# Opening of a spectral mixing and SoLU kernel: the last unit's rows, three weight loads, one conversion and the idle products are rearranged

## The chip, the cores and the metric

The kernel runs on one core of a Trainium2 chip. The metric is the device time of one execution in microseconds, as the median of five runs. The profile is of one execution of its own; its times count from the first instruction.

## The reference

Two blocks follow each other. The first filters a sequence in the frequency domain, along the sequence axis; the second is a feed-forward layer with a SoLU activation and a layer norm, over all 25088 tokens.

```python
# x: (8, 3136, 256); filt_r, filt_i: (1569, 256)
X = np.fft.rfft(x, axis=1)
Y = X * (filt_r + 1j * filt_i)[None]
y = np.fft.irfft(Y, n=3136, axis=1).reshape(25088, 256)
# w_in: (256, 1024), w_out: (1024, 256), g_ln: (1024,); both weights are float64 in memory
h = y @ w_in
e = np.exp(h - h.max(-1, keepdims=True))
solu = h * e / (e.sum(-1, keepdims=True) + 1e-9)
mu, var = solu.mean(-1), solu.var(-1)
out = (solu - mu) / np.sqrt(var + 1e-6) * g_ln @ w_out
```

## The kernel before

The Fourier transform of 3136 points is split into 49 x 64. For a batch element e there are four steps. `first` multiplies the rows by a 98 x 100 table and stores the result in DRAM (d1). `forward` (tile pb, line 300 and product at 292) takes two pairs of residues at a time, called a unit; the filter is applied in `multiply` (lines 313 to 315); `inverse` (tile pc) goes back, is evacuated by ScalarE (line 330) and stored in DRAM (d2, line 334). `back` (lines 353 and 356, tile py) loads rows of d2 as tile t4, multiplies by the table wi_t and leaves tokens in the large tile y. Batch element 0 has seven units, 0 to 6. Units 0 to 5 have four residues each; unit 6 has one residue, so its result is 128 x 256 elements, which are four rows (96 to 99) of t4.

Batch element 0 goes through all four steps in the opening (lines 360 to 560). The main loop (`step`, line 896) then runs over the token blocks: it multiplies tokens by w_in, takes the softmax, transposes, multiplies by w_out, and does the Fourier steps of the next batch elements beside it, at places that PLAN (line 37) names. The opening and the main loop are under a manual schedule: every engine runs its instructions in the order in which the code emits them, and so does each engine's DMA queue: SyncE (SP), ScalarE (ACT) and GpSimd (POOL) issue transfers. An issue on SP or ACT also waits until an earlier transfer that used the same completion semaphore has landed; eight of them go round.

What stands in the opening around the change:

- Weights. `begin(j)` issues the load of one eighth of the weights on POOL's queue (line 369, 512 KB of float64 words), j = 0 to 3 for w_in and 4 to 7 for w_out, into one of five buffers (tile raw). `convert(j)` makes float32 of it: a row of VectorE operations (lines 381 to 396), and for j below 4 also one multiplication on ScalarE (line 400) and two operations on POOL (401 and 405); for j from 4 on lines 403 on VectorE and 405 on POOL. `weight_sums` (line 141, VectorE) needs all four eighths of w_in.
- Units. The loop at line 524 emits, for unit i: the forward of unit i + 2, its multiply (real part on VectorE alone, imaginary part with its last operation, line 315, on POOL), two idle products (line 530), the inverse, and the store of the unit on ACT's queue. The tiles pr, pi, pt and g have two buffers each.
- Idle products (`idle`, line 492) write a PSUM tile that nobody reads; a row of 14 of them, tile idler, follows the last unit.
- Rows. The row loads of the step back (eight pieces, tile t; lines 172 and 173) are all issued on SP: 96 rows and 4 rows apart for each piece. After them SP issues the rows of batch element 1 (line 420, tile y), the copy of the filter to DRAM (line 548, f_dram), and then what the main loop gives it. POOL reads f_dram back at line 598, in the main loop.
- POOL makes the sums of a token pair for the main loop at line 658 (tile s), which the products on PE (line 680, tile m) need.

Of the kernel before, what the change touches and what calls it, by code (L numbers as in the profile page):

```python
# [9 lines left out]
FP32 = mybir.dt.float32  # L10
# [7 lines left out]
P = 128  # L18
B, S, C = 8, 3136, 256
# [5 lines left out]
NH = N2 // 2  # L25
# [3 lines left out]
NK = 4 * NS  # L29
NCH = 4  # L30
# [62 lines left out]
def kernel(  # L93
# [10 lines left out]
    nc = tc.nc  # L104
# [6 lines left out]
    def pool(name, bufs, space=None, stack=ctx):  # L111
        kw = {} if space is None else {"space": space}
        return stack.enter_context(tc.tile_pool(name=name, bufs=bufs, **kw))
# [7 lines left out]
    d2 = [dram.tile([NS, P, C], FP32, name=f"d2_{e}") for e in range(B)]  # L121
# [28 lines left out]
    def filter_rows(filt, quarter, u, i0, n):  # L150

        s0 = 2 * i0 + u
        off, step = (s0 * C, 2 * C) if quarter == 0 else ((N1 - s0) * C, -2 * C)
        return bass.AP(tensor=filt.tensor, offset=filt.offset + off,
                       ap=[[N1 * C, 32], [step, n], [1, C]])

    def all_filter_rows(i0, n):

        for k, filt in enumerate((filt_r, filt_i)):
            for u in range(2):  # L160
                for quarter in range(2):
                    held = min(n, (NS - u + 1) // 2 - i0)
                    yield (slice(NQ * u + 32 * quarter, NQ * u + 32 * quarter + 32), k, held,
                           filter_rows(filt, quarter, u, i0, held))

    def whole(dmas, out, in_):
        dmas[0](out=out, in_=in_)

    def by_16(dmas, out, in_):

# [164 lines left out]

    t4s = {}

    def fetch_back(e, ch, rows_pool, split=None):

        split = split or whole  # L340
        if rows_pool is not None:
            t4s[e, ch] = rows_pool.tile([P, NCH, C], FP32, name=f"t4_{e}_{ch}", tag="r")[0:NK]
        split(
            (nc.sync.dma_start if split is by_16 else nc.gpsimd.dma_start, nc.sync.dma_start), t4s[e, ch],
            d2[e].rearrange("s (a n) c -> (s a) n c", a=4)[:, NCH * ch:NCH * ch + NCH, :])

    def back(e, ch, cb, evac):

# [11 lines left out]
    with ExitStack() as st:  # L360
        fpool = pool("fp", 1, stack=st)
        pools = {name: pool(name + "0", bufs, stack=st)
                 for name, bufs in (("r", 1), ("t2", 1), ("p", 2), ("g", 2))}
# [3 lines left out]
        def load_words(src, n):  # L367
            raw = wpool.tile([P, 512, 2], I32, name=f"raw_{n}", tag="raw")
            nc.gpsimd.dma_start(
                out=raw.rearrange("p (k d) w -> p k d w", d=src.shape[-2]) if len(src.shape) == 4 else raw,  # L370
                in_=src)
            return raw
# [70 lines left out]
        def resident(held):  # L443
            def find(sp, u):
                i, pairs = sp.units[u]
                tile, at = held[i]
                return tile[:, at:at + pairs]
            return find

        sp = Spectrum(0, pools, resident(filters), resident(tables))  # L450
        raws = {}

        def begin(j):
            raws[j] = load_words(weights[j][1], j)
# [16 lines left out]
        pieces = NH // NCH  # L471
# [18 lines left out]
        def idle(out):  # L490

            nc.tensor.matmul(out=out, lhsT=tables[0][0][:, 0, 0].rearrange("p u q -> p (u q)"),
                             rhs=filters[0][0][:, 0], start=True, stop=True)

        def idle_row(count, name):
            for j in range(count):
                idle(ps_h.tile([P, 2, C], FP32, name=f"{name}_{j}", tag="h"))
# [3 lines left out]
        def convert(j):  # L501
            load_float64(weights[j][0], raws.pop(j), negate=j < 4, share=j < 4)
# [4 lines left out]
        def start(i):  # L507
            sp.fetch_filter(i)
            sp.fetch_de(i)
            sp.forward(i, halves(f"pb_0_{i}"))  # L510

        units = len(sp.units)

        sp.t2s[0] = t2_0 = pools["t2"].tile([P, 4, C], FP32, name="t2_0_0", tag="t2")
        for n in range(16):
            (nc.sync, nc.scalar)[n % 2].dma_start(
                out=t2_0[NH * (n % 4):NH * (n % 4) + NH, n // 4, :], in_=rows_x[n:n + 1])
# [6 lines left out]
        for i in range(units):  # L524
            if i + 2 < units:
                start(i + 2)
            sp.multiply(i, 0, nc.vector.tensor_tensor)
            sp.multiply(i, 1, nc.gpsimd.tensor_tensor)
            pss = [ps_t.tile([P, 2, C], FP32, name=f"pc_0_{i}_{u}", tag="t") for u in range(2)]
            idle(pss[0])  # L530
            sp.inverse(i, pss)
            sp.store(i, nc.scalar.dma_start)
            if i == 0:
                nc.gpsimd.dma_start(out=wi_t, in_=wi_dram)
                nc.gpsimd.dma_start(out=wq_t, in_=wq_dram)
                nc.gpsimd.dma_start(out=g_sb, in_=moe_g_ln.rearrange("(k p) -> p k", p=P))
            elif i != 2:
                begin({1: 2, 3: 3, 4: 4, 5: 5, 6: 6}[i])
        idle_row(14, "idler")
        rows_t4 = pools["r"].tile([P, NH, C], FP32, name="t4_0", tag="r")  # L540
        for ch in range(pieces):
            t4s[0, ch] = rows_t4[0:NK, NCH * ch:NCH * ch + NCH]
        for ch in range(pieces):
            fetch_back(0, ch, None, by_16)
        fetch_second()
        for i0, n, rows in ((0, 4, P), (4, 4, P), (8, NP - 9, P), (NP - 1, 1, NQ)):
            f, at = filters[i0]
            nc.sync.dma_start(
                out=f_dram[i0:i0 + n].rearrange("i u q k c -> (u q) i (k c)")[0:rows],
                in_=f[0:rows, at:at + n].rearrange("p i k c -> p i (k c)"))  # L550
        convert(2)
        begin(7)
        convert(3)
        convert(4)
        weight_sums(w_in_sb)
        for j in (5, 6, 7):
            convert(j)
        for ch in range(pieces):
            for cb in range(KD):
# [16 lines left out]
    pools = dict(f=pool("fp1", 2))  # L576
# [257 lines left out]
    for e in range(1, B):  # L834
        first_at, spectrum_at, back_at = PLAN[e]
        sp = Spectrum(e, pools, load_filter, load_de)
        if e == 1:
            sp = second
            sp.load, sp.load_de = load_filter, load_de
        for i, t in enumerate(first_at):  # L840
            dma = nc.gpsimd.dma_start
            if e == 1:
                if i not in sp.xs:
                    row_loads.append((t, t - 1, -1, lambda sp=sp, i=i, dma=dma: sp.fetch_x(i, [dma] * 2)))
                for u in range(2):
                    (early, late)[u][t].append(lambda sp=sp, i=i, u=u: sp.first(
                        i, (u,), psum(f"pa_{sp.e}_{i}_{u}").rearrange("p a c -> p (a c)").rearrange(
                            "p (o n) -> p o n", o=1), nc.scalar.copy, sp.xs[i][0:NK, 2 * u:2 * u + 2, :]))
                    (early, late)[u][t].append(lambda sp=sp, i=i, u=u: sp.store_first(
                        i, 2 * u, nc.gpsimd.dma_start))  # L850
            else:

                row_loads.append((t, t - 2, -1, lambda sp=sp, i=i: sp.fetch_quarters(i, nc.sync.dma_start)))
                stores[t].append(lambda sp=sp, i=i: sp.difference(i))
                products[t].append(lambda sp=sp, i=i: sp.sum(i))
                late[t].append(lambda sp=sp, i=i: sp.first_quarters(
                    i, [psum(f"pa_{sp.e}_{i}_{g}") for g in range(2)]))
                stores[t + 1].append(lambda sp=sp, i=i, dma=dma: sp.store_quarters(i, dma))
        for i, t in enumerate(spectrum_at):

            other = e == 1 and i % 2 == 1 and t + 1 < LAG
            add = nc.gpsimd.tensor_tensor if t + 1 < LAG else nc.vector.tensor_tensor


            dma = nc.sync.dma_start if e == 1 else nc.scalar.dma_start
            ahead(t, 2).append(lambda sp=sp, i=i, dma=dma: sp.fetch(i, dma))
            ahead(t, 1 if e == 1 and i % 2 == 1 else 2).append(lambda sp=sp, i=i: sp.fetch_filter(i))
            ahead(t, 2).append(lambda sp=sp, i=i: sp.fetch_de(i))
            early[t].append(lambda sp=sp, i=i, o=other: sp.forward(i, psum_pair(f"pb_{sp.e}_{i}", o)))
            late[t].append(lambda sp=sp, i=i, add=add: sp.multiply(i, 0, add))  # L870
            products[t + 1].append(lambda sp=sp, i=i, add=add: sp.multiply(i, 1, add))
            late[t + 1].append(lambda sp=sp, i=i, o=other: sp.inverse(i, psum_pair(f"pc_{sp.e}_{i}", o)))
            stores[t + 2].append(lambda sp=sp, i=i: sp.store(i, nc.gpsimd.dma_start))


        assert S * (e - 1) <= P * (back_at[0] // 2 * 2) and P * (back_at[-1] + 2) <= S * e // P // 2 * 2 * P
        for ch, t in enumerate(back_at):
            row_loads.append((
                t, t - 1, spectrum_at[-1] + 2, lambda e=e, ch=ch: fetch_back(e, ch, pools["r"])))
            for cb in range(KD):  # L880
                (early, late)[cb][t].append(
                    lambda e=e, ch=ch, cb=cb: back(e, ch, cb, nc.scalar.copy))
# [134 lines left out]
```

## Time and profile before

| what | value |
|---|---|
| median of five runs | 1684.33 us (1678.61 to 1685.2) |
| profiled execution, its own time | 1684.82 us |
| its span | 1683.0 us |
| mean granted TensorE clock | 0.988 |
| busy share: PE, DVE, POOL, ACT | 95%, 75%, 67%, 56% |
| PE busy in 0 to 100 us, and in 100 to 200 us | 71.70 us, 84.67 us |
| PE busy in 800 to 1000 us | 196.30 us |

Times in the profile are microseconds from the start of the span, where a line doesn't say ns. PE is the matrix engine, PEld its weight loads, DVE is VectorE, ACT is ScalarE, POOL is GpSimd; SPq, ACTq and POOLq are the sequencers that issue transfers. A line of the timeline has the start, the length, the engine, the line of the code, the operation, output and inputs by the program's names, shapes, how many were merged, and in brackets the idle time of the engine before it with what ended it. The chain of waits goes back from the last instruction, at each step to what released it. The page also cuts the span into 40 slices and writes the busy share of each as a digit.

### The profile page before, as it was taken

To read this page: it belongs to the slowest core of one execution; us is meant where nothing else is said; L and a number is where in the kernel's file an instruction comes from. 1 tells how busy PE (TensorE), PEld (TensorE's weight loads), DVE (VectorE), ACT (ScalarE), POOL (GpSimd) and SP (SyncE) were. 2 spreads that over 40 slices of the span, in tenths; PEclk is the share of its full clock that TensorE was granted. 3 is DMA by queue.
4 is the path that set the end of the run, shared out by engine and by line. 5 is a ranking of instruction groups with operands and counts; after the bars stand their busy time and mean duration, and the time that the engine had idled before them with its cause. 6 is when DMAs were issued, how large, how long until landed. Compare 5 with 4: busy or idle time off the path is not lost.

```text
span 1683.0 us, 31072 instructions
## 1 busy us (share of the span) xinstructions
PE 1599.5 (95%) x10022; PEld 1094.5 (65%) x10022; DVE 1267.4 (75%) x2619; ACT 939.4 (56%) x1730; POOL 1120.2 (67%) x1268
## 2 busy tenths in 40 slices
PE   5798899999999999999999999999999999999996
PEld 1353456756766677667666677667776777777776
DVE  1676787787787877887878878788778766777773
ACT  2154555656555556556565665556565666656651
POOL 4444777578666756787567866688566766666674
PEclk8998999999999999999999999999999999999999
DMA  9887768876788668865777658766776444444443
GB/s 256 247 268 223 230 195 228 215 212 173 194 230 227 184 181 232 228 184 147 202 230 211 179 151 229 226 183 173 196 210 170 116 126 123 100 109 103 112 112 96
DMA packets 375958, 311.72 MB, mean 185 GB/s; under 512 B 61515, under 2 KB 341572, under 8 KB 375796
## 3 DMA queue, kind: packets, MB, share of 16 engines
q1 hardware_dynamic: 306260, 169.81, 38.5%
q0 software_dynamic: 32640, 101.65, 20.5%
q10 hardware_dynamic: 36896, 38.28, 8.2%
q8 instruction: 81, 1.33, 0.3%
q14 instruction: 81, 0.66, 0.1%
HBM read 124.83 MB, written 81.50 MB: 123 GB/s over the span
## 4 chain that ended last, share of the span: by engine, by line
PE 64%; DMA 18%; DVE 8%; SPq 3%; issue 3%; POOL 2%; ACT 1%; ACTq 0%; DVEq 0%; POOLq 0%
PE m L680 25%; PE o L792 25%; DMA solu_t<-turn 8%; PE py L353 5%; SPq L750 2%; DMA x<-in_x_dram 2%; PE pc L292 2%; DMA t<-d 2%; PE pb L292 2%; PE pa L260 2%; DVE h L728 2%; DVE turn L738 1%; DMA out_dram<-ot 1%; DVE diff L245 1%; DMA y<-in_x_dram 1%
## 5 line engine op out<-in xcount | busy, mean ns | idle before, releaser
L730 ACT ACTIVATE e<-h,nmu 128x1024 f32<-128x1024 f32 x196 | 225.7, 1152 | 366.2 <-DVE h L728 364.2
L792 PEld LDWEIGHTS o<-w_out_sb,solu_t 128*128 128x128 f32 x3136 | 380.3, 192 | 59.3 <-issue 40.9
L792 PE MATMUL o<-w_out_sb,solu_t 128*128 128x128 f32 x3136 | 400.6, 276 | 10.2 <-DVE rsum L723 7.4
L680 PE MATMUL m<-w_in_sb,s 128*128 128x512 f32 x784 | 402.7, 605 | 6.1 <-ACT h L690 3.9
L792 PEld LDWEIGHTS o<-w_out_sb,u 128*128 128x128 f32 x2352 | 304.7, 191 | 147.1 <-issue 112.0
L658 POOL TENSOR_TENSOR u<-solu_t 128x512 f32<-128x512 f32 x98 | 145.5, 1484 | 306.1 <-DMA solu_t<-turn 186.3
L680 PE MATMUL m<-w_in_sb,y 128*128 128x512 f32 x588 | 313.1, 616 | 15.8 <-DVE nmax L704 11.9
L792 PE MATMUL o<-w_out_sb,u 128*128 128x128 f32 x2352 | 312.4, 276 | 6.8 <-ACT ot L804 5.8
L728 DVE SCALAR_TENSOR_TENSOR h<-e,rsum,h 128x1024 f32<-128x1024 f32 x196 | 291.1, 1485 | 6.9
L811 DVE SCALAR_TENSOR_TENSOR ot<-o,rs_t,ot 128x128 f32<-128x128 f32 x294 | 102.6, 349 | 202.4 <-ACT ot L804 166.6
L690 ACT COPY h<-m 128x512 f32<-128x512 f32 x294 | 173.9, 591 | 128.3 <-PE m L680 115.5
L738 DVE STREAM_TRANSPOSE turn<-h 128x1024 f32<-128x1024 f32 x196 | 242.3, 1236 | 0.8
L712 ACT ACTIVATE e<-h,nmax 128x1024 f32<-128x1024 f32 x196 | 226.5, 1155 | 0.0
L658 POOL TENSOR_TENSOR u<-solu_t,u 128x512 f32<-128x512 f32 x98 | 142.8, 1457 | 89.9 <-PE o L792 86.0
L704 DVE CUSTOM_DVE_ANT_0 h<-m,h 128x512 f32<-128x512 f32 x196 | 133.2, 680 | 78.2 <-ACT h L690 58.2
L680 PEld LDWEIGHTS m<-w_in_sb,y 128*128 128x128 f32 x588 | 94.9, 191 | 124.8 <-DVE nmax L704 65.6
L680 PEld LDWEIGHTS m<-w_in_sb,s 128*128 128x128 f32 x784 | 124.1, 191 | 67.6 <-issue 44.9
L356 ACT COPY y<-py 128x392 f32<-128x392 f32 x128 | 109.5, 856 | 104.7 <-PE py L353 102.9
L353 PEld LDWEIGHTS py<-wi_t,t 100*128 100x128 f32 x1024 | 132.2, 192 | 54.2 <-issue 40.5
L658 POOL TENSOR_TENSOR solu_t<-solu_t,solu_t 128x512 f32<-128x512 f32 x98 | 150.0, 1530 | 7.7
L658 POOL TENSOR_TENSOR u<-u,solu_t 128x512 f32<-128x512 f32 x98 | 136.2, 1390 | 0.7
L353 PE MATMUL py<-wi_t,t 100*128 100x98 f32 x1024 | 131.7, 273 | 0.7 <-DMA t<-d 0.4
(108 smaller groups left out, 1986.3 us busy)
## 6 DMA issues: line engine op xcount, KB each, us to landing
solu_t<-turn SPq DMA_DIRECT2D x784, 128.0 KB
out_dram<-ot SPq DMA_DIRECT2D x196, 128.0 KB
t<-d POOLq DMA_DIRECT2D x56, 400.0 KB, 5.0
d<-x POOLq DMA_DIRECT2D x100, 200.0 KB, 5.3
f<-f_dram POOLq DMA_DIRECT2D x39, 512.0 KB, 7.2
d<-g POOLq DMA_DIRECT2D x39, 512.0 KB, 5.3
t<-d ACTq DMA_DIRECT2D x36, 512.0 KB
x<-in_x_dram SPq DMA_DIRECT2D x112, 98.0 KB
```

What stands on the lines that cost most here:

```text
L353: nc.tensor.matmul(out=psv[:, i:2 * NCH - i:2 * NCH - 1 - 2 * i, :], lhsT=t4s[e, ch][:, i, cb * P:cb * P + P], rhs=wi_t, start=True, stop= ...
L356: evac(out=y[:, cb, t0:t0 + S].rearrange("p (r m j) -> p m j r", m=N2 // NCH, j=NCH)[:, ch:last + 1 - ch:last - 2 * ch], in_=psv.rearrange ...
L658: nc.gpsimd.tensor_tensor(out=out, in0=in0, in1=in1, op=op)
L680: nc.tensor.matmul(out=ms[j, bank], lhsT=lhsT, rhs=w_in_sb[:, w, :], start=m in (1, 2, 7), stop=True, skip_group_check=True)
L690: nc.scalar.copy(out=h_half(k, i), in_=ms[j, 0])
L704: nc.vector.tensor_tensor_reduce(out=h_half(k, i), in0=ms[j, bank], in1=h_half(*kept), scale=1.0, scalar=sofar, op0=ALU.add, op1=ALU.min, ...
L712: nc.scalar.activation(out=e, in_=hs[k], func=AFT.Exp, bias=nmaxs.pop(k)[:, 1:2], scale=-1.0, accum_out=esum)
L728: nc.vector.scalar_tensor_tensor(out=solu, in0=e, scalar=rsum, in1=solu, op0=ALU.mult, op1=ALU.mult, accum_out=nmu)
L730: nc.scalar.activation(out=e, in_=solu, func=AFT.Square, bias=nmu, scale=-float(DFF), accum_out=variances[g][:, i:i + 1])
L738: nc.vector.transpose(out=turns[g][:, :, i, :], in_=solus.pop(k).rearrange("p (f j) -> p f j", j=32))
L792: nc.tensor.matmul(out=pos[p, bank], lhsT=lhs[:, f, :], rhs=w[:, f, :], start=f == 0 and m in (1, 2, 7), stop=True, skip_group_check=True)
L811: nc.vector.scalar_tensor_tensor(out=ot, in0=pos[p, bank], scalar=rs, in1=out_half(p, *kept)[0], op0=ALU.mult, op1=ALU.add)
```

## The change

Six things are changed in the opening; the main loop is the same.

1. The store of unit 6 to DRAM is gone. Its four rows of t4 are written by four transfers straight from the tile g, each from 32 partitions into one row, two on ACT's queue and two on SP's.
2. The row loads of the step back are the 96-row ones alone, on SP behind those two.
3. Conversion 2 is emitted at the end of unit 2's turn, in place of after the row loads. Load 2 is issued at unit 0 and no longer at unit 1.
4. Loads 5, 6 and 7 are issued together after conversion 3. Before, 5 and 6 were issued at units 5 and 6, and 7 after conversion 2.
5. Conversion 4 comes after the weight sums and no longer before them; the loads of wi, wq and g come at unit 1 instead of unit 0.
6. The row of idle products has 9 instead of 14.

```diff
             idle(pss[0])
             sp.inverse(i, pss)
-            sp.store(i, nc.scalar.dma_start)
-            if i == 0:
+            if i + 1 < units:
+                sp.store(i, nc.scalar.dma_start)
+            if i in (0, 3, 4):
+                begin({0: 2, 3: 3, 4: 4}[i])
+            elif i == 1:
                 nc.gpsimd.dma_start(out=wi_t, in_=wi_dram)
                 nc.gpsimd.dma_start(out=wq_t, in_=wq_dram)
                 nc.gpsimd.dma_start(out=g_sb, in_=moe_g_ln.rearrange("(k p) -> p k", p=P))
-            elif i != 2:
-                begin({1: 2, 3: 3, 4: 4, 5: 5, 6: 6}[i])
-        idle_row(14, "idler")
+            elif i == 2:
+                convert(2)
+        idle_row(9, "idler")
         rows_t4 = pools["r"].tile([P, NH, C], FP32, name="t4_0", tag="r")
+        last = sp.gs.pop(units - 1)
+        for a in range(4):
+            (nc.scalar, nc.sync)[a % 2].dma_start(out=rows_t4[NK - 4 + a:NK - 3 + a],
+                                                  in_=last[NH * a:NH * a + NH, 0, :])
         for ch in range(pieces):
             t4s[0, ch] = rows_t4[0:NK, NCH * ch:NCH * ch + NCH]
-        for ch in range(pieces):
-            fetch_back(0, ch, None, by_16)
+            nc.sync.dma_start(
+                out=t4s[0, ch][0:NK - 4],
+                in_=d2[0].rearrange("s (a n) c -> (s a) n c", a=4)[0:NK - 4, NCH * ch:NCH * ch + NCH, :])
         fetch_second()
...
-        convert(2)
-        begin(7)
         convert(3)
-        convert(4)
+        for j in (5, 6, 7):
+            begin(j)
         weight_sums(w_in_sb)
-        for j in (5, 6, 7):
+        for j in range(4, 8):
             convert(j)
```

The function `whole` and the split of `fetch_back` go, since nothing else used them; for batch elements 1 to 7 `fetch_back` issues the same transfer as before.

## The prediction

> **What bounds the kernel now.** I read the page first: TensorE (PE) is busy for 95% of the span, and the 40 slices show a 9 for nearly all of it but the first four. The change touches only the opening, so I went to the table of 10 us windows for 0 to 200 us, where PE is busy for 156 of 200 us: there is slack there, and the question is which chain of waits holds it. Then I read the chain of waits over 55 to 120 us:
>
> ```profile
> 72.83 1.12 PE pc L492 x2
> 73.96 1.11 PE pc L292 x16
> 75.09 0.60 ACT g L330
> ...
> 78.88 1.12 PE pc L492 x2
> 80.01 0.58 PE pc L292 x4
> 80.59 12.21 PE idler L492 x28
> 92.80 1.09 PE py L353 x8
> ```
>
> The columns are start, length, work. A unit of the spectrum takes 2.9 to 3.1 us on PE (72.83 to 75.73 to 78.88); after the last one the 14 idle products run for 12.21 us (0.872 each), and the step back (py) starts at 92.80, the moment they end. They cover the row loads, which come late for this reason (first the waits of SyncE's queue, then the DMA queues in 80 to 84 us; the columns of the second are packets, MB and share of 16 engines):
>
> ```profile
> SPq L172 <- DMA d<-g: 21.1, 3, 10.6
> ```
> ```profile
> q0 software_dynamic: 220, 0.82, 77.4%
> q10 hardware_dynamic: 103, 0.10, 6.9%
> ```
>
> SP waits for the stores of the units. Unit 5's store is issued at 79.35, SP gets on at 88.03: 8.7 us, because in between GpSimd's queue (weight loads 5 and 6, issued at 77.03 and 78.89) moves 0.82 MB and the store's queue 0.10. From 88 us to 145 us the SP queue then always has work, and its end decides the next thing that stops PE, read in POOL's and PE's timelines:
>
> ```profile
> 141.12 0.74 POOL L598 DMA_DIRECT2D f<-f_dram  x1 [6.66 <-DMA f_dram<-f]
> 141.87 0.88 POOL L658 TENSOR_TENSOR s<-y 128x128 f32<-128x128 f32 x1
> ```
> ```profile
> 144.43 2.04 PE L680 MATMUL m<-w_in_sb,s 128*128 128x512 f32 x2 [3.27 <-ACT h L690]
> ```
>
> POOL waits 6.66 us for the filter's copy to DRAM (f_dram, line 548, behind the rows and the second batch element on SP's queue); its sums for the next token pair stand behind that, and PE waits 3.27 us. So the opening has two clocks: PE's (units, idle products, step back) and SP's DMA stream.
>
> **The change, part by part.** All times below are of the profiled execution: 1684.82 us, of which the span is 1683.0. It lies 0.49 above the median of the five runs (1684.33), so I add my sum to the median.
>
> *Conversion 2 between units 2 and 3.* It leaves VectorE's (DVE's) row behind unit 6 (77.95 to 82.50, 4.55 us) and enters a hole:
>
> ```profile
> 66.12 0.69 DVE L313 TENSOR_TENSOR pr<-pb,f 128x512 f32<-128x512 f32 x1 [6.91 <-PE pc L292]
> ```
>
> DVE idles 6.91 us up to 66.12. Load 2 is issued at 54.06 instead of 57.36; the six late loads land 4.5 to 8.4 us after issue, so at 58.6 to 62.5, and DVE is through by 63.8 to 67.1: nothing to 0.9 us late, taken as 0. But the conversion also has a multiplication on ScalarE (ACT, line 400, 0.69) and two operations on POOL (401 and 405, 1.46 and 1.35), and engines run them in the order written. ACT's one stands behind the evacuation and store of unit 2, and POOL's two stand ahead of unit 3's last operation (line 315):
>
> ```profile
> 70.29 0.37 ACTq L334 DMA_DIRECT2D d<-g  x1
> ```
> ```profile
> 69.48 1.27 POOL L315 TENSOR_TENSOR pi<-pi,pt 128x512 f32<-128x512 f32 x1 [8.86 <-DVE pt L314]
> ```
>
> So line 400 runs 70.70 to 71.39, 401 to 72.85, 405 to 74.2, and unit 3's line 315 ends at 75.4 instead of 70.75. PE's second half of inverse 3 (8 products, 1.09 us at unit 0) ends at 76.5, not 72.2: 4.3 us late. PE and DVE both need about 3 us a unit, so nothing is caught up. DVE's next pi also waits, since its pt buffer is freed by that line 315, and unit 5 waits for buffers of unit 3. On top, PE stands still from about 72.0 to 75.4. A gap of this kind is in the trace: 2.55 us before line 292 at 165.17, also waiting for POOL's pi, with a granted clock of 0.83 in 160 to 170 us; after 4.93 us of idling it was 0.71 in 60 to 70, where a pair of idle products took 2.00 instead of 1.05 and an inverse 1.87 instead of 1.04. That adds 0 to 2.5 us; I take 0.7. Delay of the units: 5.0 us (4.3 to 6.8; 0 to 1 if the order doesn't bind).
>
> The Trainium skill, "TensorE: Matmul & The Clock Gate", section "Why this matters for your kernels", wants no idle gaps above about 3 us. By it a gap of 3.4 us would cost clock and one of 2.55 would not; the rows at 165 us show that one of 2.55 did, and the sum changes by no more than the 0.7.
>
> *Nine idle products.* Five fewer: 5 x 0.872 = 4.36 us off PE, in full if the rows are there. The last inverse ends at 80.6 + 5.0 = 85.6, nine take 7.85, so the step back could start at 93.45, against 92.80: +0.65.
>
> *Last unit's rows directly.* Removed are unit 6's store on ACT, its way through DRAM and SP's eight 4-row loads (16 KB each, 0.28 to 0.33 us of SP); added are four SBUF copies of 32 KB (two on ACT, two on SP ahead of the row loads). The main loads wait for unit 5 already, and unit 6's evacuation ends at 81.4 + 5.0 = 86.4, before they can go (next part), so SP loses nothing. The trace has such copies only the other way (t<-x, 32 KB): 3.23 us in the chain of waits, 9.65 behind a backlog. The rows would be there at 90.0 to 96.4: 0 to 2.9 us of waiting. I take 0, by the 3.23, as only one store stands ahead. On ACT the conversion of load 3 stands behind the two issues (0.7 us); DVE is later than that.
>
> *Three loads later.* Loads 5, 6 and 7 go from 77.03, 78.89 and 85.80 to behind conversion 3 on POOL. Unit 5's store, now undisturbed, needs about 3.7 us (67.28 to 70.70 and 70.29 to 74.12 for units 1 and 2): issued at 84.35, landed at 88.0. SP starts where it did (88.03). But two loads, 1.05 MB, that were through by then now lie on top of the row loads: at 250 GB/s, the rate of 88 to 102 us, that is 4.2 us of DMA; the 0.13 MB of removed 4-row loads give back 0.5. SP's stream is 3.7 us later, f_dram with it; I take 3.0, since in 102 to 112 us the DMA engines are only 47% busy (bounds 0 and 4.2). Will the loads be late for DVE? Conversion 3 ends at about 88 on DVE, and POOL issues load 5 at about 89.4; it lands by 97.8 at worst, when conversion 5 is due at 97: 0 to 1.
>
> *DVE's sum.* Unit 6 ends 4.7 later; 4.55 of conversion 2 are gone; conversion 3 shrinks from 6.99 to about 5.0, as POOL's work on conversion 2 is no longer beside it; conversion 4 no longer covers POOL's 1.35 us before the weight sums, +1. Net -0.8, and POOL's first sums (116.81) with it: no bound.
>
> *wi, wq and g* are loaded one unit later (57 instead of 54), with the first use at 92.8: nothing.
>
> **Sum.** Step back +0.65; DVE -0.8; SP's stream +3.0, and this one decides at 141 us, when POOL gets on at 144.1. What follows is the same code, shifted. +3.0: 1684.33 + 3.0 = 1687.3.
>
> **The rivals.**
>
> *The conversion hides, and the opening is shorter.* If unit 3 is delayed by 1 us or less (for it speaks that POOL idles 8.86 us before 69.48), the step back starts at 92.80 - 4.36 + 1 = 89.45 and SP at about 84. The stream then ends 4.0 earlier and 3.7 later, so f_dram is about even, and the gain of 3.4 counts only if POOL's wait shrinks: 1680.9. Against it stands the order on ACT.
>
> *The weight loads starve the rows.* This is the slower side. At 80 to 84 us GpSimd's queue took 0.82 of 0.92 MB. If it does so again, the three loads (1.57 MB, 6.3 us) hold up the row loads that follow the first; these had 0.7 us of margin in the second piece and 2.7 in the last (from landing to the step back's 2.08 us a piece). PE would stand 4 to 6 us within the step back, with a halved clock behind it, and the stream ends 6 later: about +8, 1692. It decides from about 80% of the engines for GpSimd's queue; at half each, as in 118 to 130 us (0.54 against 0.46 at 122), the margins hold.
>
> The Trainium skill, "DMA: Bandwidth & Descriptors", section "Queues, rings and completion order", says that each DMA engine takes turns between queues packet by packet, which would mean halves and no more than the forecast. The 77.4% against 6.9% contradict this; I keep both.
>
> *Nothing reaches the end.* All shifts meet the wait at 141 us, which stays where it was: 1684.3.
>
> **How the numbers follow.** Forecast 0.45, hidden conversion 0.22, starved rows 0.20, nothing 0.13. 0.3% is 5.05 us, about what a measurement of this kernel can tell from no change. Faster by that takes half of the second case: 0.11. Slower takes five sixths of the starved rows and a fifth of the forecast (clock and stream at their upper bounds): 0.26. Between: 0.63. The range reaches from the hidden conversion's 1680.9 less 0.9 for the unknown landing, 1680.0, to the starved rows' 1692 and a half, 1692.5.
>
> **What would show it.** Unit 3's line 315 at about 74.2 with ACT's line 400 at 70.7 ahead of it; a PE gap of over 3 us before inverse 3; last inverse near 85.6, step back near 93.5; SP's first row load near 88; POOL's line 598 near 144. The forecast is wrong if line 315 of unit 3 still runs at 69.5, if the row pieces come over 3 us apart, or if line 598 doesn't move with the SP stream.

## The result and the profile after

| | before | after |
|---|---|---|
| median | 1686.45 us (89 runs beside the changed kernel) | 1692.32 us (47 runs) |
| ratio, 95% interval | 1 | 1.0035 [1.0026, 1.0045] |
| profiled execution, its own time | 1684.82 us | 1696.4 us |
| its span | 1683.0 us | 1694.6 us |
| mean granted TensorE clock | 0.988 | 0.979 |
| last inverse done, step back starts, products for the first tokens start | 80.6, 92.80, 109.43 us | 90.3, 98.55, 117.21 us |
| SP's first row load | 88.03 us | 92.09 us |
| POOL's line 598 (now 601) | 141.12 us | 146.53 us |

The change costs 5.9 us (4.4 to 7.6), 0.35%; the forecast was 3.0. The profiled execution of the changed kernel lies 4.1 above its own median, that of before 1.6 below the median of the 89 runs, so the 11.6 us between the two profiles are not the change's. From profile to profile the stretch from the 12th to the 196th transpose of the main loop, which is the same code, took between 1398.8 and 1415.0 us over the kernels of this study, with no visible relation to the opening. So in what follows the runs' medians say what an edit costs, and the profiles say only where in the opening it costs it. Lines of the changed kernel's helpers and units lie 3 to 5 lower: 312 is the old 315, 395, 396 and 400 the old 400, 401 and 405, 327 the old 330, 487 the old 492, 348 the old 353; 683 is the old 680.

The order of conversion 2 is the first thing to look at. POOL's timeline of the changed kernel over 66 to 78 us, and after it ACT's:

```profile
73.00 1.29 POOL L396 TENSOR_TENSOR raw<-raw,power 128x512 f32<-128x512 f32 x1 [13.18 <-ACT raw L395]
74.37 1.28 POOL L400 TENSOR_TENSOR w_in_sb<-w_in_sb,raw 128x512 f32<-128x512 f32 x1
75.60 1.26 POOL L312 TENSOR_TENSOR pi<-pi,pt 128x512 f32<-128x512 f32 x1
```
```profile
67.66 1.07 ACT L327 COPY g<-pc 128x512 f32<-128x512 f32 x2 [11.89 <-PE pc L289]
...
71.78 0.37 ACTq L331 DMA_DIRECT2D d<-g  x1
72.24 0.68 ACT L395 ACTIVATE raw<-raw 128x512 f32<-128x512 int32 x1 [0.50 <-DVE pt L311]
```

Unit 3's last operation on POOL (312) follows the conversion's two, these follow ACT's 395, and this stands behind unit 2's evacuation and store, step by step as the diff made one expect. POOL idled 13.18 us ahead of 73.00. Measured from the start of unit 1's evacuation on ACT, which is in the block above at 67.66 and was here before:

```profile
66.18 1.07 ACT L330 COPY g<-pc 128x512 f32<-128x512 f32 x2 [9.82 <-PE pc L292]
```

the operation ran 3.3 us later before (66.18 to 69.48) and runs 7.9 later now (67.66 to 75.60): the order costs 4.6 us. PE stood still for it, by its timeline:

```profile
76.92 0.49 PE L289 MATMUL pc<-pi,de 64*64 64x256 f32 x2 [3.36 <-POOL pi L312]
```

The chain of waits then shows what that sets off:

```profile
75.60 1.27 POOL pi L312
76.88 0.04 issue
76.92 0.49 PE pc L289 x2
...
79.34 2.08 PE pc L487 x2
81.42 2.00 PE pc L289 x16
83.42 0.02 issue
83.44 0.60 ACT g L327
...
88.55 1.12 PE pc L487 x2
```

The pair of idle products took 2.08 us and an inverse 2.00; before it was 1.12 and 1.11, and at 88.55 it is 1.12 again. The table of windows for the same stretch (span, then busy time of PE, PEld, DVE, ACT and POOL, the granted clock, the DMA share and GB/s):

```profile
77.00:87.50 10.50, 9.12 (x48) 3.42 (x48) 7.38 (x14) 2.15 (x4) 4.41 (x5) 0.51 0.64 201
```

Against it the same part of the kernel before:

```profile
69.00:81.00 12.00, 10.35 (x85) 4.65 (x81) 11.76 (x22) 4.30 (x9) 7.29 (x8) 1.00 0.85 268
```

So what is left of unit 3, unit 4 and most of unit 5 run at half clock, for ten microseconds. From line 312 of unit 3 to the end of the last inverse it is 14.6 us, before 11.1: +3.5. Then the step back, in PE's timeline:

```profile
90.18 7.99 PE L487 MATMUL idler<-f,de 128*128 128x512 f32 x18
...
98.55 12.42 PE L348 MATMUL py<-wi_t,t 100*128 100x98 f32 x96 [0.38 <-DMA t<-d]
112.11 5.31 PE L348 MATMUL py<-wi_t,t 100*128 100x98 f32 x32 [1.14 <-DMA t<-d]
117.21 3.67 PE L683 MATMUL m<-w_in_sb,y 128*128 128x512 f32 x4
```

It starts when the nine products end, waits 1.14 us for its last pieces of rows, and takes 18.7 us instead of 16.6. Last, DVE, whose rows were to be 0.8 us earlier:

```profile
95.73 2.02 DVE L141 TENSOR_TENSOR w_in_sb<-w_in_sb 128x512 f32<-128x512 f32 x3 [5.51 <-POOL w_in_sb L400]
...
105.26 0.43 DVE L376 TENSOR_SCALAR raw<-raw 128x512 int32<-128x512 int32 x1 [3.43 <-DMA raw<-in_moe_w_out_dram]
...
121.02 0.69 DVE L707 CUSTOM_DVE_ANT_0 h<-m,h 128x512 f32<-128x512 f32 x1 [1.24 <-issue]
```

The same row maximum before:

```profile
112.37 0.68 DVE L704 CUSTOM_DVE_ANT_0 h<-m,h 128x512 f32<-128x512 f32 x1
```

It loses 5.51 us to POOL's part of conversion 3 and 3.43 to load 5, and ends its last conversion at about 119.8 (before: 112.4). The row maximum for the first tokens (line 707) stands behind that, but in this execution DVE was idle for 1.24 us ahead of it: the products that it reads ended at 120.88, so PE's delay held it, and DVE's own did not. At 141 us, where the forecast had put the decision, the wait is gone (POOL's timeline):

```profile
146.53 0.76 POOL L601 DMA_DIRECT2D f<-f_dram  x1
```

No idle time in front of it and no f_dram: what stands before it on POOL now is the first step's own stores.

### The profile page after: what moved, and what is told of

The parts are those of the page before. It is cut to its first block, busy times and chain, and to the rows that moved or that the text cites. A ratio compares the mean times of both kernels' runs of the same rounds, so it can differ in the third digit from the quotient of the medians.

```text
span 1694.6 us, 31042 instructions
## 1 busy us (share of the span) xinstructions
PE 1605.3 (95%) x10012; PEld 1098.5 (65%) x10012; DVE 1263.6 (75%) x2619; ACT 938.4 (55%) x1730; POOL 1118.4 (66%) x1268
## 4 chain that ended last, share of the span: by engine, by line
PE 66%; DMA 15%; DVE 8%; issue 3%; SPq 3%; ACT 2%; POOL 2%; ACTq 0%; DVEq 0%; POOLq 0%
PE o L795 27%; PE m L683 26%; DMA solu_t<-turn 6%; PE py L348 5%; SPq L753 3%; PE pa L257 2%; PE pc L289 2%; PE pb L289 2%; DMA t<-d 2%; DMA out_dram<-ot 2%; DVE h L731 2%; PE pa L214 2%; DVE turn L741 1%; DVE diff L242 1%; DMA t<-x 1%
## 5 line engine op out<-in xcount | busy, mean ns | idle before, releaser
L795 PE MATMUL o<-w_out_sb,solu_t 128*128 128x128 f32 x3136 | 401.4, 276 | 11.4 <-DVE rsum L726 8.3
L661 POOL TENSOR_TENSOR u<-solu_t 128x512 f32<-128x512 f32 x98 | 141.5, 1444 | 311.4 <-DMA solu_t<-turn 198.4
L683 PE MATMUL m<-w_in_sb,y 128*128 128x512 f32 x588 | 317.2, 623 | 14.7 <-DVE nmax L707 12.1
```

What stands on the lines that cost most here:

```text
L661: nc.gpsimd.tensor_tensor(out=out, in0=in0, in1=in1, op=op)
L683: nc.tensor.matmul(out=ms[j, bank], lhsT=lhsT, rhs=w_in_sb[:, w, :], start=m in (1, 2, 7), stop=True, skip_group_check=True)
L795: nc.tensor.matmul(out=pos[p, bank], lhsT=lhs[:, f, :], rhs=w[:, f, :], start=f == 0 and m in (1, 2, 7), stop=True, skip_group_check=True)
```

## The experiments

Each time is a ratio to the kernel before on the same chip, with its 95% interval; 0.1% is 1.7 us. Stretches named in microseconds are those of one profiled execution.

### Is it the place of conversion 2? Three ways to undo it

**Back to its old place** (a1_conv_back, against the changed kernel):

```diff
-            elif i == 2:
-                convert(2)
...
+        convert(2)
         convert(3)
```

> The changed kernel with conversion 2 emitted after the row loads again, right before conversion 3; the rest of the change stays. Theory of the order (ScalarE's part of conversion 2 stands behind the evacuation of unit 2, so GpSimd's last operation of unit 3 comes 4 to 5 us late and the clock halves): that operation is back at 70 to 71 us, the last inverse ends at 81 to 83 instead of 90.3, the step back starts at 89 to 91, and the time is 5 to 8 us below the changed kernel, within 2 us of the kernel before. Theory of the starved rows (loads 5 to 7 lie on the row loads): the units are on time too, but the step back waits for its rows, and the time stays 4 us or more above the kernel before.

Measured 1.0006 [0.9985, 1.0028]. Unit 3's line 312 runs at 68.0, the last inverse ends at 79.1, the step back runs from 87.4 to 104.0: 5.4 us earlier than before the change. And then PE stands still:

```profile
87.44 16.59 PE L348 MATMUL py<-wi_t,t 100*128 100x98 f32 x128 [0.39 <-DMA t<-d]
...
114.27 4.90 PE L214 MATMUL pa<-y,wf_t 98*100 98x512 f32 x6 [7.25 <-DVE nmax L706]
```

It waits 7.25 us for the row maximum on DVE, which stands in the midst of the last conversion. That chain lost 1.19 us on the weight sums and then waited for load 5 (DVE's timeline):

```profile
100.04 0.43 DVE L376 TENSOR_SCALAR raw<-raw 128x512 int32<-128x512 int32 x1 [4.45 <-DMA raw<-in_moe_w_out_dram]
...
113.53 0.68 DVE L706 CUSTOM_DVE_ANT_0 h<-m,h 128x512 f32<-128x512 f32 x1
```

So the order costs about what the theory says (4.9 us by the two ratios, 5 to 8 expected), and the rest of the change gains nothing, as the earlier step back meets a later DVE.

**Ahead of unit 2's inverse** (a2_conv_ahead, the same operations):

```diff
             sp.multiply(i, 1, nc.gpsimd.tensor_tensor)
+            if i == 2:
+                convert(2)
...
-            elif i == 2:
-                convert(2)
```

> The changed kernel with the same operations, conversion 2 emitted within unit 2's turn ahead of the inverse and its evacuation instead of behind the store, so that ScalarE's multiplication stands ahead of unit 2's evacuation (but behind unit 1's). Theory of the order: unit 3's last operation comes 2 to 4 us earlier than in the changed kernel relative to unit 1's evacuation, the time is 2 to 5 us below the changed kernel (1.0005 to 1.0025). If the order on ScalarE is not what counts, the time is that of the changed kernel, 1.0025 or more.

Measured 1.0010 [0.9992, 1.0028]. ACT's 395 now runs at 64.12, ahead of unit 2's evacuation, and POOL is through sooner (ACT's timeline, then POOL's):

```profile
64.12 0.70 ACT L395 ACTIVATE raw<-raw 128x512 f32<-128x512 int32 x1 [0.53 <-ACT g L327]
```
```profile
64.90 1.75 POOL L396 TENSOR_TENSOR raw<-raw,power 128x512 f32<-128x512 f32 x1 [5.14 <-ACT raw L395]
66.73 1.29 POOL L400 TENSOR_TENSOR w_in_sb<-w_in_sb,raw 128x512 f32<-128x512 f32 x1
67.97 1.76 POOL L312 TENSOR_TENSOR pi<-pi,pt 128x512 f32<-128x512 f32 x1
```

Line 312 comes 5.5 us after unit 1's evacuation starts, against 7.9 in the changed kernel; the last inverse ends at 80.6. By the two ratios (1.0035 and 1.0010, whose intervals just overlap) the same work in the same unit costs some 4 us less by where it stands on ACT. All three ways keep load 2 at its early place, unit 0, so the earlier load is not what costs.

**Without ACT** (a3_no_act; the multiplication of conversion 2 on VectorE, in place of one on ACT and one on POOL):

```diff
-            load_float64(weights[j][0], raws.pop(j), negate=j < 4, share=j < 4)
+            load_float64(weights[j][0], raws.pop(j), negate=j < 4, share=j < 4 and j != 2)
```

> The changed kernel with conversion 2 at its new place, but its multiplication by a power of two on VectorE, as the conversions from 4 on have it, so that ScalarE has no part in it and GpSimd only the last addition. Theory of the order: GpSimd's addition runs near 65 us, unit 3's last operation near 71, the last inverse ends at 81 to 83, and the time is 5 to 8 us below the changed kernel. If it were the place of the conversion on VectorE or its load's traffic that delays the units, the last inverse would stay near 90 and the time within 2 us of the changed kernel.

Measured 1.0009 [0.9991, 1.0026]. Line 312 at 68.37 (4.1 after the evacuation), the last inverse at 79.5, the step back from 87.8. This one then runs into the rows: its pieces stop at 100.2, PE waits 1.84 us at 102.04, the clock halves up to 111.8, and the step back ends at 109.2, 21.4 us after its start.

### Each part alone, put into the kernel before

**The conversion alone** (b1_conv_only, with load 2 at unit 0 and the tables at unit 1):

```diff
-            if i == 0:
+            if i == 1:
...
             elif i != 2:
-                begin({1: 2, 3: 3, 4: 4, 5: 5, 6: 6}[i])
+                begin({0: 2, 3: 3, 4: 4, 5: 5, 6: 6}[i])
+            else:
+                convert(2)
...
-        convert(2)
         begin(7)
```

> The kernel before with conversion 2 between units 2 and 3 alone (load 2 issued at unit 0 and the three small tables at unit 1, as in the changed kernel); 14 idle products, the rows through DRAM and loads 5 to 7 as before. Theory of the order: unit 3's last operation on GpSimd at 74 to 76 us, last inverse at 85 to 90, and the time 4 to 9 us above the kernel before. Theory of the starved rows: no more than 2 us above.

Measured 1.0028 [1.0008, 1.0048]: most of the change's loss, from this edit by itself. Line 315 of unit 3 at 73.4, 8.0 after unit 1's evacuation, a PE gap of 3.37 us ahead of 74.71, half clock to 81.7, last inverse at 86.6, step back from 98.62 to 115.1.

**The same without ACT** (d4_before_no_act, b1 with the edit of a3):

> The kernel before with conversion 2 between units 2 and 3 (load 2 at unit 0, small tables at unit 1) and its multiplication on VectorE; all else as before. Theory of the order: unit 3's last operation is no longer held (within 3 us after the wait for unit 3's rows, as in the kernel before), and the time lies 2 to 5 us below the same kernel with ScalarE's part (1.0028), so 0.998 to 1.001 of the kernel before. If the earlier load 2 is what delays the units, it stays at 1.002 or more.

Measured 1.0021 [0.9999, 1.0042]: this doesn't tell. In its profile the units are on time (315 of unit 3 at 68.1, last inverse at 79.2, the 12th transpose 4.3 us earlier than before), so the opening did what the theory says, and the time didn't: the main loop of that execution took 1415 us, before's 1402.

**The three loads alone** (b2_loads_only):

```diff
-            elif i != 2:
-                begin({1: 2, 3: 3, 4: 4, 5: 5, 6: 6}[i])
+            elif i in (1, 3, 4):
+                begin({1: 2, 3: 3, 4: 4}[i])
...
-        begin(7)
         convert(3)
+        for j in (5, 6, 7):
+            begin(j)
```

> The kernel before with loads 5, 6 and 7 issued after conversion 3 alone. Theory of the order: units as before, SyncE's first row load 3 to 5 us earlier (83 to 85 us), the later row pieces slower by the loads; the time within 2 us of the kernel before. Theory of the starved rows: the step back stands 4 to 6 us for its rows and the time is 4 to 8 us above the kernel before.

Measured 1.0019 [1.0001, 1.0037]. Without the loads SP gets on 6.8 us earlier (81.27; before 88.03), and the rows were not starved: the step back ran from 91.7 to 108.2. The loss stands behind it, in PE's timeline:

```profile
91.72 16.50 PE L353 MATMUL py<-wi_t,t 100*128 100x98 f32 x128
...
114.58 3.74 PE L217 MATMUL pa<-y,wf_t 98*100 98x512 f32 x4 [3.34 <-DVE nmax L705]
```

DVE again: it waited 2.1 us for load 5.

**The direct rows alone** (b3_rows_only; the store of unit 6 and the 4-row loads go, as in the diff of the change):

> The kernel before with the last unit's rows copied directly and the 96-row loads alone; loads, conversions and 14 idle products as before. SyncE waits for unit 5's store before and after (near 88 us), so the step back stays at 92 to 93; the eight 4-row loads (0.13 MB) go from the row stream, which may give 0 to 1 us. Time within 2 us of the kernel before. If the direct copies into one row were slow (over 9 us, as the slowest of the copies at the start), the step back would start after 94 and the time be 1 to 3 us above.

Measured 0.9999 [0.9979, 1.0019]: free, within 0.2%. (In its profile the wait of PE for y<-d ahead of unit 3 was 8.1 us instead of 4.9, which moved all that follows; over the profiles of this study it was 2.9 to 8.5, without relation to the edit.)

**The nine products alone** (b4_nine_only):

```diff
-        idle_row(14, "idler")
+        idle_row(9, "idler")
```

> The kernel before with 9 in place of 14 idle products. If the rows set the start of the step back, it starts at 92 to 93 as before, after a gap of about 4 us on PE, and the first part of the step back runs at half the clock: 0 to 4 us above the kernel before. If the idle products set it, it starts near 89 and the time is up to 3 us below.

Measured 1.0042 [1.0026, 1.0058]: an edit that only takes away work nobody reads, and it costs more than any other part, and more than the 4 us expected at most. The rows of before come later than nine products end (PE's timeline, then the windows of its step back):

```profile
80.35 7.99 PE L492 MATMUL idler<-f,de 128*128 128x512 f32 x18
91.66 27.60 PE L353 MATMUL py<-wi_t,t 100*128 100x98 f32 x128 [3.32 <-DMA t<-d]
```
```profile
92.00:119.00 27.00, 27.00 (x128) 27.00 (x128) 19.30 (x32) 12.69 (x15) 8.44 (x8) 0.50 0.83 261
```

The windows of the kernel before, for the same 128 products:

```profile
92.80:109.40 16.60, 16.24 (x128) 14.91 (x128) 16.22 (x27) 12.96 (x15) 4.49 (x3) 1.00 0.79 212
```

The step back starts 1.1 us earlier and takes 11 us longer. PE stood idle for 3.32 us, and then worked without a pause at half the clock until the step back was over; the full clock came back at 121.4, 30.7 us after it had gone.

### What do the nine save in the changed kernel?

**Fourteen in the changed kernel** (d1_fourteen; `idle_row(9, "idler")` becomes `idle_row(14, "idler")`):

> The changed kernel with 14 idle products again, nothing else. If in the changed kernel the rows come as the nine end (profile: products end at 98.2, step back starts at 98.6), five more put 4.4 us on PE: 2 to 5 us above the changed kernel, 1.005 to 1.007 of the kernel before. If the nine leave PE idle and the clock down in the step back in a part of the executions, as they do in the kernel before with nine alone, 14 take nothing or give up to 3 us: 1.002 to 1.0035.

Measured 1.0049 [1.0029, 1.0069], against 1.0035 for nine: nine save about 2.4 us here, though the two intervals overlap. The five products are 4.3 us; with fourteen the rows have more time, and the step back runs through in 16.5 us (102.0 to 118.5) where with nine it took 18.7. By these figures about half of the five products' time is given back to the rows and the clock. The granted clocks agree: their mean over the 10 runs with fourteen is 0.984, over those of the changed kernel 0.981.

### Can what is left of the gain be had?

If the step back of a1 and a3 is 5 us earlier and DVE's chain spoils it, DVE's chain is what to mend.

**Loads one by one** (c1_staggered, against a3):

```diff
         convert(3)
-        for j in (5, 6, 7):
-            begin(j)
+        begin(5)
+        convert(4)
+        begin(6)
         weight_sums(w_in_sb)
-        for j in range(4, 8):
-            convert(j)
+        convert(5)
+        begin(7)
+        convert(6)
+        convert(7)
```

> The changed kernel with ScalarE out of conversion 2 (as the run with its multiplication on VectorE), conversion 4 ahead of the weight sums, and the loads 5, 6 and 7 issued one by one after conversions 3, 4 and 5. Theory (order on ScalarE and GpSimd, then the loads in one bunch on the rows and VectorE's waits for them): VectorE loses its waits for the weight sums (3.1 us) and for load 5 (3.5 us), the step back runs in 17 to 19 us in place of 21, the conversions end at 104 to 107, and the time is 2 to 6 us below the kernel before. If the main loop's first steps are held by something else (SyncE's stream), it is within 2 us of the kernel before.

Measured 1.0019 [0.9999, 1.0039]: missed. The step back was as good as it gets (87.6 to 104.1), but DVE still waited for two loads:

```profile
94.19 0.43 DVE L376 TENSOR_SCALAR raw<-raw 128x512 int32<-128x512 int32 x1 [3.49 <-DMA raw<-in_moe_w_out_dram]
...
107.68 0.43 DVE L376 TENSOR_SCALAR raw<-raw 128x512 int32<-128x512 int32 x1 [4.14 <-DMA raw<-in_moe_w_out_dram]
```

Load 5 took 9.4 us to land, beside the rows. The last conversion ended at 111.7, the row maximum behind it at 112.38, and PE stood still up to 112.42:

```profile
112.42 5.44 PE L214 MATMUL pa<-y,wf_t 98*100 98x512 f32 x6 [5.37 <-DMA f_dram<-f]
```

The line names a piece of f_dram that landed at 112.41, after the row maximum by 0.02 us, so this profile can't tell which of the two held PE. In a1 and b2 PE also starts 0.04 us after the row maximum.

**Loads 5 and 6 early again** (c2_loads_early, against a3):

```diff
-            if i in (0, 3, 4):
-                begin({0: 2, 3: 3, 4: 4}[i])
+            if i in (0, 3, 4, 5, 6):
+                begin({0: 2, 3: 3, 4: 4, 5: 5, 6: 6}[i])
...
-        for j in (5, 6, 7):
-            begin(j)
+        begin(7)
```

> The changed kernel with ScalarE out of conversion 2 and loads 5 and 6 issued at units 5 and 6, as before the change, 7 after conversion 3. Unit 5's store is held up by the loads again (5 us), SyncE's first row load is near 86 and PE waits 2 to 4 us after the nine idle products; VectorE no longer waits for load 5. If loads on the rows cost more than loads on the store, the time is 1 to 4 us below the run with the multiplication on VectorE; if less, above it.

Measured 1.0074 [1.0049, 1.0098], the slowest of all. Now the loads lie ahead of unit 5's store, SP's first row load comes at 93.5, PE waits 4.62 us ahead of the step back, and this takes 27.6 us at half clock, as in b4.

**The same with fourteen products** (d2_early_fourteen):

> The changed kernel with ScalarE out of conversion 2, loads 5 and 6 at units 5 and 6, and 14 idle products. Theory (the loads on unit 5's store make the rows late by about 5 us, and what nine products then cost is the halved clock through the whole step back): the clock stays full in the step back, which takes 16 to 18 us in place of 28, and the time falls by 9 to 13 us from the same kernel with nine, to within 3 us of the kernel before. If the early loads cost by something else, it stays at 1.005 or more of the kernel before.

Measured 1.0033 [1.0001, 1.0065] without the longest run, 6 us below c2 by the medians, where 9 to 13 were expected. The twelve times lie in two groups with nothing between them, six from 1680.8 to 1686.4 and six from 1696.9 to 1706.9. The profiled execution is one of the upper: its rows came 1.8 us after the products' end, and its windows are those of b4:

```profile
95.00:122.00 27.00, 26.90 (x129) 26.82 (x130) 12.83 (x22) 12.84 (x16) 2.81 (x2) 0.52 0.82 267
```

The mean granted clock of each execution tells the groups apart: 0.985 to 0.989 in the lower six, 0.976 to 0.978 in the upper six, as in all of c2 (0.976 to 0.978). At half clock for 27.3 us of 1700 the mean falls by 0.008, so the upper group is the one with the slow step back, and the ratio of 1.0033 is a mixture of the two. That the lower group's rows came in time is not shown, as no profile of it exists.

## Why the prediction was right in its direction and short in its size

**What it had right.** The order on ACT and POOL: line 312 delayed by 4.6 us (4.7 forecast), with ACT's 395 ahead of it, and a PE gap of 3.36 us (3.4 forecast). Undone in three ways, the loss goes from 0.35% to 0.06 to 0.10%, by 4 to 5 us; by itself it makes 0.28% [0.08, 0.48]. The direct rows cost nothing by themselves (b3), and came 5.75 us after their issue, between the two ends given. Conversion 2 fits the hole on DVE. Unit 5's store took no more than 3.1 us, from 89.01 to SP's first row load (3.7 forecast). The rival in which the conversion hides fell, and so did the one in which nothing reaches the end. Of the 5.0 us between 1687.3 and the measured 1692.3, 2.1 are the base, which was 1684.33 over five runs and 1686.45 over 89.

**"That adds 0 to 2.5 us; I take 0.7": the mis-sized term.** The half clock behind the gap of 3.36 us cost 3.5 us in this profile and 2.1 in b1's (13.2 us from line 315 of unit 3 to the last inverse, against 11.1). The prediction named two rows for it (0.71 in 60 to 70 us, 0.83 in 160 to 170) and gave no working from them to 0.7. What counts is how long the clock stays down, and it stayed down for 10.2 us here and 6.8 in b1 and d1, behind gaps of 3.36, 3.37 and 3.35 us. So even the same gap has more than one price, and one profile doesn't give it. The step back's start follows: forecast 93.45, measured 98.55. Of the 5.1 between, 3.2 lie from line 312 to the last inverse (14.6 against 11.4 forecast; 2.8 of them are the clock term), 1.4 are that line 312 came at 75.60 and not 74.2, as everything from unit 1's evacuation on was 1.5 later behind a y<-d wait of 7.47 us (before 4.93), which varies without relation to the edit, and the rest is the 0.38 us for rows and nine products of 7.99 instead of 7.85.

**"DVE -0.8": wrong by its sign.** The sum said that ACT's part of conversion 3 behind the two direct copies does no harm, as "DVE is later than that". DVE had its part of conversion 3 done at 89.6, ACT's 395 ran at 92.30, POOL's two up to 95.7, and the weight sums waited 5.51 us where 1 was forecast. It is the same mistake as the one the prediction found for conversion 2, one conversion later: ACT's operation of a conversion stands behind the last evacuation (90.32; before 81.00), and this had moved by 9.3 us. Then load 5 was late by 3.43 (forecast 0 to 1). In the changed kernel this lateness was hidden, as the row maximum waited for PE. a1 and b2 show its price where loads 5 to 7 are late and the step back is not: PE waits 7.3 and 3.3 us for the row maximum behind DVE's conversions, and in c1 5.4, where f_dram is named beside it. In d4, with these loads at their old place, the step back ends at 107.7 and PE has no such wait.

**"SP's stream +3.0, and this one decides at 141 us": wrong.** POOL came to line 601 at 146.53 with no wait. The step back and DVE were already 7.8 and 7.4 us late at 117 to 120 us, and this delay is carried on: the 12th transpose is 9.1 us later, the 196th 8.4. So the 3.0 came out of the wrong chain. By the prediction's own reading of the other two, PE's step back was to cost 0.65 and DVE to gain 0.8; that the sum still had the right sign is luck in this part.

**The starved rows** came in a small form: 1.14 us of waiting at 112.11 and a halved clock behind it, 2.1 us in the step back and some 1.5 in the four products after it (3.67 us, at full clock 2.2 in a1), of the 8 that this rival gave; 1.84 us and some 5 in a3. That d1 gives half of its five products back fits this. It depends on how the rows arrive, and these are at the edge. The weight loads are not the only thing that delays them. The prediction had SP lose nothing to the direct rows, but SP's waits have

```profile
SPq L546 <- DMA t<-g: 2.1, 1, 2.1
```

The last four row loads went out only when a direct copy had landed (96.48), and the one issued at 97.31, which PE waited for at 112.11, took 14.66 us to land. How much of PE's 1.14 us is the copy's and how much the loads', no run divides. The prediction also read the 77.4% against 6.9% as speaking against turns packet by packet. Its two lines give 220 packets of 3.7 KB on average against 103 of 1.0 KB, so a good part of that difference is the size of the packets; no run here tests how the queues take turns.

**Do the parts make the sum?** Conversion 4 to 5 us, loads 3.2 (b2), rows 0, nine products -2.4 (d1): 5 to 6 us, against 5.9 measured. Each of these has an uncertainty of about 3 us, and they are not independent: nine products alone cost 7 us in the kernel before and save 2 in the changed one. So the agreement is no proof that nothing else takes part. Still open are why the y<-d wait ahead of unit 3 varies so much, d4's time, and what the places of conversion 4 and of the small tables cost, which were not changed alone.

One thing that the text on the kernel has too strictly: an engine's order is not everywhere the order in the code. In the changed kernel POOL makes the sums of the first pair (118.38) ahead of the last conversion's line 400 (120.88), and in a1 the row maximum stands inside conversion 7. For conversion 2 and unit 3 the two orders agree.

## What to carry to other kernels

Work moved into an engine's idle hole brings its other engines' parts along: look up, for each operation of the moved step, what stands ahead of it in that engine's order and how late that already is; here one 0.68 us operation on ACT, put ahead of the evacuation instead of behind it, was worth about 4 us. When several chains end within a microsecond or two of each other (here the step back at 109.4 and DVE's conversions at 112.4), speeding up one is worth little, and the sum has to be made for each chain to its end. Filler products are priced by whether the data is there when they end: five fewer saved about 2 us where nearly all rows were in time, and cost 7 where the first were not.

## What the runs showed of the hardware

A stretch of products can stay at half clock for as long as it lasts. In b4, c2 and d2 PE idled 1.8 to 4.6 us just ahead of the step back; its 128 products (100 rows, 98 columns) then ran for 27 us at a granted clock of 0.50 to 0.52 with PE busy all the time, while with no such gap the same products ran at 1.00 from the first to the last. The Trainium skill, "TensorE: Matmul & The Clock Gate", section "What's actually happening", says that the full clock returns after about 3.4 us of sustained activity. The windows of b4 do not fit it, if a busy PE is such activity: 27.00 us busy of 27.00, at 0.50. In the units of the changed kernel, with wider products and short pauses, the clock did come back, after 10.2 us. What counts as activity no run here settles.

The half clock comes and goes in steps of 3.41 us. Over the first 200 us of all 14 profiles its stretches lasted 3.41, 6.83, 10.24, 13.65, 27.31 or 30.72 us, whole multiples of the first, and within one execution their starts lie whole multiples apart too. So a gap is priced in steps: those of 3.35 to 3.37 us cost two (b1, d1) or three (the changed kernel).

Three weight loads issued together on GpSimd's queue beside the row loads needed 9.6 to 16.1 us each to land (the changed kernel, a1, a2, a3, b2, d1), and one by one in c1 8.0 to 9.4, against 4.5 to 8.4 for those from 57 to 86 us in the kernel before.
